# Four stages turned by DMA transposes instead of TensorE, in a fused recurrence and feed-forward kernel

## The chip, the cores and the metric

The kernel runs on one core of a Trainium2 chip. The metric is the device time of one execution in microseconds (us); lower is better. The value is the median over the timed runs.

## The reference

A linear recurrence with a decay per channel (an RWKV layer), followed by a feed-forward layer with a leaky ReLU:

```python
batch, n_heads, seq, head_dim = (4, 8, 768, 48)
for t in range(S):
    kt, vt, rt = (k[:, :, t].copy(), v[:, :, t].copy(), r[:, :, t].copy())
    cur = np.einsum('bhd,bhe->bhde', u[None] * kt, vt)
    y[:, :, t] = np.einsum('bhd,bhde->bhe', rt, state + cur)
    state = w[None, :, :, None] * state + np.einsum('bhd,bhe->bhde', kt, vt)
...
n_tokens, d_model, d_ff = (3072, 384, 2048)
h = x @ w_in
g = np.maximum(0.01 * h, h)
return (g @ w_out).astype(np.float32)
```

x is y with the heads side by side: 3072 tokens by 384 channels. Inputs and output are float32; the kernel computes in bfloat16 with float32 sums.

## The kernel before

The recurrence is computed in chunks of 128 tokens. There are 24 stages; stage n is chunk n // 4 of batch n % 4, so four neighbouring stages belong to four different batches, and stage n hands its state to stage n + 4. Each stage goes through these steps, and each step has a letter, by which an order of work written out by hand names it:

- r, k, v: loads of the stage's three inputs. GpSimd (POOL) issues them, converting to bfloat16, except stage 0's r and k (SP and ACT). wi and wo with a number are quarters of the two weight matrices, also issued by GpSimd.
- P (q or k): DVE multiplies r or k with a table of decay powers (qtab, ktab), giving the tile qk.
- The tile is turned so that channels lie on partitions (tile tp). Either TensorE (PE) does it, four matmuls against the identity for each half (T), and ACT or, with an @ behind the name, DVE copies the result from PSUM (t); or, with X and T around the number (X8T), one DMA transpose issued by SP does the whole stage.
- A: PE computes the products of q and k of a chunk into two PSUM banks. M (a or b): DVE masks one bank above the diagonal into the tile at.
- The diagonal (the term with u) has two forms. In the first, X without T multiplies the turned halves (prod) on DVE, D sums them over channels with wu on PE, Q scales v by the sums on DVE (vs), and Y begins with three matmuls of vs. M is then a multiplication by the mask. In the second, q is three DVE instructions (row_sums, which need the table u_tab), Q is two GpSimd instructions that put the sums on the diagonal of at, and M copies the products over it by predicate, so that it waits for Q; Y has no matmuls of vs.
- K: PE multiplies k and v. S: DVE makes the next state of it. Y: PE computes the stage's output, from stage 4 on with the state; y: ACT copies it to xT.
- G n.g and g n.g: a group of four blocks of the first feed-forward matrix for one stage on PE, and its activation on ACT. J m.j and j m.j: two blocks for a pair of stages. H and h: the second matrix for one stage on PE, its copy on ACT and its store by SP.
- F with a number: so many matmuls of ones on PE, without use for the result.

Before the change, stages 0 to 7 are turned by PE and have the first form of the diagonal (TURNED, DIAG = 8, 8); stages 8 and later use the transpose and the second form. The table u_tab is made from one row of u: SP loads the row, ACT converts it (u16), PE spreads it over partitions (U), ACT copies it (utab).

Everything up to stage 5's first feed-forward half is listed in ORDER, a string of these names. Each engine does its own steps in the order of that string, and a step waits by semaphore only for what it reads or overwrites. PSUM has 8 banks, handed out in rotation in the order of the list. After the list a loop runs over pairs of stages, m from 3 to 11: J for the pair m, then the sums and diagonals of the next but one pair, loads of later stages, P and transposes, H for the pair before, A, Y, M, K and S. The loop's text is the same for all stages.

GpSimd's queue matters here: it issues all loads but two and computes the diagonals of the second form, one after the other. SP's queue carries the transposes and stores.

Of the kernel before, what the change touches and what calls it, by code (L numbers as in the profile page):

```python
# [7 lines left out]
AF = mybir.ActivationFunctionType  # L8
AX = mybir.AxisListType
BF16 = mybir.dt.bfloat16  # L10
FP32 = mybir.dt.float32
# [6 lines left out]
HD = H * D  # L18
# [4 lines left out]
NSL = HD // 128  # L23

FIRST, NB, PACE = 6, B, 3
TURNED, DIAG, CARRY, EXACT = 8, 8, 4, 1
ORDER = """
w k0 r0 w8 u8 u wlz tcol k1 ones table one exps qk0 r1 v0z r5 F12 bc wi2 lnw id qtab wu8 v0 id8 u16 F13 Cm P0q ktab U
k3 P1q T0q Wl P0k utab T1q r3 P1k t0q T0k C P5q W T1k t1q@ k4 T5q t0k t1k@ tri t5q F2 A0 X0 v1 X1 F2 A1 M0a F3 D0 wi1
M0b F5 D1 F1 K0 k5 P3k P3q F11 T3k Q0 r4 F3 T3q P4k t3k F3 Y0 M1b v3 t3q T4k M1a y0 F2 K1 A3 r2 t4k Q1 F1 G0.2 M3a wi3  # L30
F1 Y1 S1 g0.2 G0.1 M3b v5 y1 X3 F2 G1.2 r7 P5k g0.1 S0 T5k g1.2 D3 P4q k6 G1.1 Q3 t5k T4q r6 g1.1 K3 P2q Y3 S3 t4q T2q
k2 X5 y3 F2 A5 X4 F1 A4 t2q M5a G3.2 v4 M4b F1 G3.3 wi0 g3.2 M4a D4 D5 G0.3 g3.3 k7 M5b G1.3 P7q g0.3 v7 Q5 K5 P6k G3.1
g1.3 S5 wo2 T6k g3.1 Y5 P6q v2 P2k t6k T6q Q4 y5 r10 F2 K4 T2k t6q@ T7q t2k Y4 v6 t7q@ A6 y4 S4 F1 A2 wo3 G1.0 M6a r11
F1 J2.7 P7k g1.0 M6b wo0 J2.0 j2.7 M2b J2.6 v8 j2.0 X2 M2a J2.2 j2.6 wo1 K7 J2.1 j2.2 v9 S7 K2 J2.4 j2.1 S2 r9 G0.0
P10q j2.4 r8 K6 J2.3 g0.0 S6 v11 D2 G3.0 j2.3 X6 Q2 k8 T7k g3.0 D6 J2.5 Q6 t7k k11 Y2 P11q j2.5 X7 A7 k9 y2 Y6 M7a k10
D7 M7b y6 G2.1 Q7 v10 G2.0 g2.1 G2.3 g2.0 G2.2 g2.3 H1 g2.2 P9q P8q H2 h1 P8k q8 X8T K8 H0 h2 P9k Q8 S8 X9T P10k P11k
K9 X10T H3 h0 q9 X11T S9 Q9 Y7 h3 A9 y7 A8 M8a M9a M9b M8b k12 r12 v12 k13 r13 v13
"""


# [4 lines left out]
class Sched:  # L45
# [7 lines left out]

    def add(self, eng, emit, R=(), W=(), dma=None):
        o = Op()
        o.eng, o.emit, o.dma, o.inc, o.val = eng, emit, dma, False, None
        deps = []
        for key in R:
            w = self.writer.get(key)
            if w is not None:  # L60
                deps.append((w, True))
        for key in W:
            w = self.writer.get(key)
            if w is not None:
                deps.append((w, False))
            for r in self.readers.get(key, ()):
                deps.append((r, False))
        o.deps = []
        for d, raw in deps:
            if d.dma is None and d.eng == eng and dma is None and (eng == "pe" or not raw):  # L70
                continue
            if d is not o and d not in o.deps:
                o.deps.append(d)
        for key in R:
            self.readers.setdefault(key, []).append(o)
        for key in W:
            self.writer[key] = o
            self.readers[key] = []
        self.ops.append(o)
        return o  # L80
# [47 lines left out]
def bass_rwkv5_eagle__then__act_leaky_relu_kernel(  # L128
# [13 lines left out]
    def SB(name, shape, dt=BF16):  # L142
        return ctx.enter_context(nc.sbuf_tensor(name, shape, dt))
# [5 lines left out]
    k_sb = SB("k_sb", [128, NST, HD])  # L149
    v_sb = SB("v_sb", [128, NST, H * E])  # L150
    w_row = SB("w_row", [128, HD // 2], FP32)
    u_row = SB("u_row", [1, HD], FP32)
    one_row = SB("one_row", [128, 128], FP32)
    u_row16 = SB("u_row16", [1, HD])
    w_head = SB("w_head", [H, D], FP32)
    u_head = SB("u_head", [H, D], FP32)
    wu_head = SB("wu_head", [H, D], FP32)
# [3 lines left out]
    lnw = SB("lnw", [128, HD], FP32)  # L161
    u_tab = SB("u_tab", [128, HD])
    k_f = SB("k_f", [128, EXACT, HD], FP32)
    r_f = SB("r_f", [128, EXACT, HD], FP32)
    qtab = SB("qtab", [128, HD])
    ktab = SB("ktab", [128, HD])
    tcol = SB("tcol", [128, 1], FP32)
# [4 lines left out]
    ones = SB("ones", [128, 128])  # L172
# [17 lines left out]
    V, A, PE, SP, G = nc.vector, nc.scalar, nc.tensor, nc.sync, nc.gpsimd  # L190
    sch = Sched(ctx, nc)
    add = sch.add
    free = list(range(8))

    def take():
        i = free.pop(0)
        return ps[i], ("ps", i)

    def give(key):
        free.append(key[1])  # L200

    def dram(h, offset, pattern):
        return bass.AP(tensor=h.tensor, offset=h.offset + offset, ap=pattern)
# [12 lines left out]
    def load_one(n, which, pace=()):  # L216
# [4 lines left out]
        else:  # L221
            dst = {"k": k_sb, "r": r_sb}[which][:, n, :].rearrange("p (h d) -> p h d", d=D)
        add("pool", lambda: G.dma_start(dst, src), R=pace, W=[(which, n)], dma=f"{which}{n}")  # L223

# [12 lines left out]
        add("pool", lambda: G.dma_start(w_out_sb[:, 4 * i:4 * i + 4, :], wout_view[:, 4 * i:4 * i + 4, :]),  # L237
            W=[("wout", i)], dma=f"wout{i}")

    def row(h):  # L240
        return dram(h, 0, [[HD, 1], [1, HD]])

    def by_head(h):
        return dram(h, 0, [[D, H], [1, D]])
# [11 lines left out]
    def fill(n):  # L256
# [6 lines left out]

        add("pe", emit, R=["ones"], W=[("ps", i), f"fill{n}"])

    def identity():
        add("pool", lambda: G.affine_select(ident[:, :], ones[:, 0:128], pattern=[[1, 128]], compare_op=ALU.is_equal,
                                            fill=0.0, base=0, channel_multiplier=-1), R=["ones"], W=["ident"])

# [52 lines left out]
        add("dve", lambda: V.tensor_tensor(wu_head[:, :], w_head[:, :], u_head[:, :], ALU.mult),  # L322
            R=["w_head", "u_head"], W=["wu_head"])

    def u_cast():
        add("act", lambda: A.activation(u_row16[:, :], u_row[:, :], AF.Copy), R=["u_row"], W=["u_row16"])

    def u_spread():
        ps_u, key = u_bank["u"] = take()
        add("pe", lambda: PE.matmul(ps_u[:, 0:HD], ones[0:1, 0:128], u_row16[:, :], start=True, stop=True),  # L330
            R=["ones", "u_row16"], W=[key])

    def u_table():
        ps_u, key = u_bank["u"]
        add("act", lambda: A.activation(u_tab[:, :], ps_u[:, 0:HD], AF.Copy), R=[key], W=["u_tab"])
        give(key)

    u_bank, c_bank = {}, {}
    at_bank, kv_bank, y_bank = {}, {}, {}

    def hd(x):
# [316 lines left out]
    def g2_out(n, c0=0, c1=HD):  # L658
# [14 lines left out]
            W=["w_row"], dma="w"),  # L673
        "w8": lambda: add("sp", lambda: SP.dma_start(w_head[:, :], by_head(w)), W=["w_head"], dma="w8"),
        "u8": lambda: add("sp", lambda: SP.dma_start(u_head[:, :], by_head(u)), W=["u_head"], dma="u8"),
        "u": lambda: add("sp", lambda: SP.dma_start(u_row[:, :], row(u)), W=["u_row"], dma="u"),
        "one": lambda: add("dve", lambda: V.memset(one_row[:, :], 1.0), W=["one_row"]),
        "tcol": tokens, "ones": filled, "exps": exponents, "v0z": zero_v, "qk0": zero_qk, "wlz": zero_w,
        "id": identity, "tri": triangle, "table": preload, "id8": small_identity, "wu8": wu_product,
        "bc": spread_w, "lnw": log_w, "qtab": lambda: table(qtab, qexp, "q"), "ktab": lambda: table(ktab, kexp, "k"),  # L680
        "Cm": columns_mm, "Wl": log_columns, "C": decay_columns, "W": decay_table,
        "u16": u_cast, "U": u_spread, "utab": u_table,
    }
    stage = {
        "P": lambda n, x: prep_half(n, half_of[x]), "T": lambda n, x: turn_mm(n, half_of[x]),
# [108 lines left out]
```

## Time and profile before

| | |
|---|---|
| median of the runs | 172.35 us (171.53 to 172.49, 3 runs) |
| span of the profiled execution | 168.6 us |
| its own time beside the span | not recorded; the span runs from the first to the last instruction, and the median is 3.75 us above it |
| PE busy | 163.7 us, 97% |
| DVE, ACT, POOL busy | 106.9, 90.8, 103.6 us |
| granted TensorE clock | 1.000 |

In the profile, PE is TensorE's matmuls, PEld its weight loads, DVE VectorE, ACT ScalarE, POOL GpSimd and SP SyncE; a q behind a name is the engine's issue queue. L with a number is a line of the kernel. A row of grouped instructions has line, engine, operation, output<-input, shapes and count, and behind the bar busy us, mean ns of one, and idle time of the engine before it with what ended it. A row of the chain has start, length and what. A row of the windows view has the window and its length, the busy time and count of PE, PEld, DVE, ACT and POOL in turn, then the granted clock, DMA packets in work (as a multiple of the 16 engines) and GB/s.

### The profile page before, as it was taken

To read this page: it belongs to the slowest core of one execution; us is meant where nothing else is said; L and a number is where in the kernel's file an instruction comes from. 1 tells how busy PE (TensorE), PEld (TensorE's weight loads), DVE (VectorE), ACT (ScalarE), POOL (GpSimd) and SP (SyncE) were. 2 spreads that over 40 slices of the span, in tenths; PEclk is the share of its full clock that TensorE was granted. 3 is DMA by queue.
4 is the path that set the end of the run, shared out by engine and by line. 5 is a ranking of instruction groups with operands and counts; after the bars stand their busy time and mean duration, and the time that the engine had idled before them with its cause. 6 is when DMAs were issued, how large, how long until landed. Compare 5 with 4: busy or idle time off the path is not lost.

```text
span 168.6 us, 5011 instructions
## 1 busy us (share of the span) xinstructions
PE 163.7 (97%) x2170; PEld 126.1 (75%) x2170; DVE 106.9 (63%) x217; ACT 90.8 (54%) x167; POOL 103.6 (61%) x117
## 2 busy tenths in 40 slices
PE   6899999999999999999999999999999999999994
PEld 4787898988667867867867867768768668668663
DVE  6599799874583999869959959969876050000000
ACT  3837866886123933933834735735637538449221
POOL 7999999990249998994993993993708100000000
PEclk9999999999999999999999999999999999999999
DMA  6999999999999959999599399299241011011012
GB/s 99 142 151 165 170 167 173 182 184 148 130 167 187 163 75 144 155 118 173 71 140 167 64 141 177 71 132 193 59 121 47 0 51 47 0 51 47 29 68 95
DMA packets 99148, 19.67 MB, mean 117 GB/s; under 512 B 92339, under 2 KB 99126, under 8 KB 99126
## 3 DMA queue, kind: packets, MB, share of 16 engines
q0 software_dynamic: 76512, 10.03, 92.1%
q1 hardware_dynamic: 21574, 9.12, 23.2%
q8 instruction: 17, 0.28, 0.7%
q10 hardware_dynamic: 1040, 0.20, 0.6%
q14 instruction: 5, 0.04, 0.1%
HBM read 20.45 MB, written 4.72 MB: 149 GB/s over the span
## 4 chain that ended last, share of the span: by engine, by line
PE 89%; POOL 5%; DMA 4%; issue 0%; ACT 0%; POOLq 0%
PE ps L652 37%; PE ps L628 31%; PE ps L605 6%; PE ps L566 6%; DMA w_in_sb<-in_moe_w_in_dram 4%; PE ps L432 4%; PE ps L473 2%; POOL k_sb L223 2%; POOL r_sb L223 2%; PE ps L407 1%; POOL v_sb L223 1%; PE ps L559 1%; PE ps L261 0%; POOL w_in_sb L233 0%; PE ps L460 0%
## 5 line engine op out<-in xcount | busy, mean ns | idle before, releaser
L652 PE MATMUL ps<-w_out_sb,gT 128*128 128x384 bf16 (+2 forms) x400 | 65.7, 320 | 0.0
L628 PE MATMUL ps<-xT,w_in_sb 128*128 128x256 bf16 x480 | 54.7, 273 | 0.0
L652 PEld LDWEIGHTS ps<-w_out_sb,gT 128*128 128x128 bf16 x400 | 37.9, 98 | 22.0
L393 POOL TENSOR_TENSOR at<-ident,s_tok 128x512 bf16<-128x512 bf16 x32 | 35.0, 1121 | 26.9 <-DVE s_tok L386 26.9
L628 PEld LDWEIGHTS ps<-xT,w_in_sb 128*128 128x128 bf16 x480 | 46.6, 98 | 6.4 <-ACT xT L580 0.2
L638 ACT ACTIVATE gT<-ps 128x512 bf16<-128x512 f32 x80 | 47.8, 597 | 6.4 <-PE ps L628 1.6
L664 ACT ACTIVATE out_sb<-ps 128x384 f32<-128x384 f32 (+2 forms) x25 | 11.9, 478 | 52.9 <-PE ps L652 52.9
L445 DVE CAST_PREDICATED at<-mask,ps 128x512 bf16<-128x512 uint16 x32 | 19.8, 684 | 18.0 <-PE ps L432 18.0
L223 POOL DMA_DIRECT2D v_sb<-in_v_dram x24 | 22.9, 955 | 0.0
L223 POOL DMA_DIRECT2D k_sb<-in_k_dram x23 | 21.5, 965 | 0.4 <-issue 0.4
L223 POOL DMA_DIRECT2D r_sb<-in_r_dram x23 | 21.2, 930 | 0.0
L353 DVE TENSOR_TENSOR qk<-r_sb,qtab 128x384 bf16<-128x384 bf16 x23 | 14.2, 617 | 3.8 <-DMA r_sb<-in_r_dram 3.8
L353 DVE TENSOR_TENSOR qk<-k_sb,ktab 128x384 bf16<-128x384 bf16 x23 | 13.0, 570 | 1.3 <-DMA k_sb<-in_k_dram 1.3
L580 ACT ACTIVATE xT<-ps 128x384 bf16<-128x384 f32 x24 | 11.0, 491 | 4.8 <-PE ps L566 4.8
L605 PE MATMUL ps<-xT,w_in_sb 128*128 128x128 bf16 x192 | 12.5, 219 | 0.4 <-DMA w_in_sb<-in_moe_w_in_dram 0.4
L615 ACT ACTIVATE gT<-ps 128x512 bf16<-128x512 f32 x16 | 9.6, 597 | 5.3 <-PE ps L605 4.9
L605 PEld LDWEIGHTS ps<-xT,w_in_sb 128*128 128x128 bf16 x192 | 11.0, 98 | 0.8 <-DMA w_in_sb<-in_moe_w_in_dram 0.5
L384 DVE TENSOR_TENSOR rku<-r_sb,ku 128x384 bf16<-128x384 bf16 x16 | 10.8, 675 | 0.6
L566 PE MATMUL ps<-at,v_sb 128*32 128x128 bf16 x384 | 10.8, 220 | 0.0
L534 DVE TENSOR_TENSOR sum_t<-ps,st 128x384 bf16<-128x384 f32 x16 | 8.8, 551 | 2.7 <-PE ps L473 2.7
L441 DVE TENSOR_TENSOR at<-ps,mask 128x512 bf16<-128x512 f32 x16 | 10.3, 681 | 0.3 <-PE ps L432 0.3
L261 PE MATMUL ps<-ones 128*128 128x128 bf16 x69 | 8.5, 257 | 1.3 <-DVE ones L251 1.3
(60 smaller groups left out, 135.1 us busy)
## 6 DMA issues: line engine op xcount, KB each, us to landing
out_dram<-out_sb SPq DMA_DIRECT2D x23, 192.0 KB, 3.6
v_sb<-in_v_dram POOLq DMA_DIRECT2D x24, 96.0 KB, 6.3
k_sb<-in_k_dram POOLq DMA_DIRECT2D x23, 96.0 KB, 6.1
r_sb<-in_r_dram POOLq DMA_DIRECT2D x23, 96.0 KB, 5.9
w_in_sb<-in_moe_w_in_dram POOLq DMA_DIRECT2D x4, 384.0 KB, 6.8
w_out_sb<-in_moe_w_out_dram POOLq DMA_DIRECT2D x4, 384.0 KB, 9.3
tp<-qk SPq DMA_TRANSPOSE x16, 2.8
k_f<-in_k_dram ACTq DMA_DIRECT2D x1, 192.0 KB, 2.7
```

Source lines behind the costliest of these rows:

```text
L223: add("pool", lambda: G.dma_start(dst, src), R=pace, W=[(which, n)], dma=f"{which}{n}")
L353: add("dve", lambda: V.tensor_tensor(qk[iq][:, H * half:H * half + H, 0:D], hd(src), hd(tab[:, :]), ALU.mult), R=[(name, n), "qk"[half] + ...
L384: add("dve", lambda: V.tensor_tensor(rku[i2][:, :], r_of(n), ku[i2][:, :], ALU.mult), R=[("r", n), ("ku", i2)], W=[("rku", i2)])
L393: add("pool", lambda hh=hh, s_of=s_of: G.tensor_tensor(at[ia][:, hh, :, :], ident[:, :].unsqueeze(1).to_broadcast([128, NP, 128]), s_of.un ...
L445: add("dve", lambda: V.copy_predicated(at[n % NAT][:, hh, :, :], mask[:, :].bitcast(mybir.dt.uint16).unsqueeze(1).to_broadcast([128, NP, 1 ...
L566: last = PE.matmul(ps_y[32 * q:32 * q + 32, 128 * s:128 * s + 128], a, m, start=not whole and step == 0, stop=step == len(columns[q]) - 1)
L580: add("act", lambda: A.activation(xT[m % NX][:, :, 128 * half:128 * half + 128], ps_y[:, 0:HD].rearrange("p (s t) -> p s t", t=128), AF.Copy),
L605: last = PE.matmul(ps_g[:, 128 * f:128 * f + 128], w_in_sb[:, s, 128 * fb:128 * fb + 128], xT[ix][:, s, t], start=s == 0, stop=s == NSL - 1)
L628: last = PE.matmul(ps_g[:, 256 * f:256 * f + 256], w_in_sb[:, s, 128 * fb:128 * fb + 128], xT[ix][:, s, :], start=s == 0, stop=s == NSL - 1)
L638: add("act", lambda: A.activation(gT[ig][:, 2 * j:2 * j + 2, :].rearrange("p f t -> p (f t)"), ps_g[:, :], AF.Prelu, alpha=0.01), R=[key], ...
L652: last = PE.matmul(ps_o[:, 0:c1 - c0], gT[ig][:, s, 128 * half:128 * half + 128], w_out_sb[:, s, c0:c1], start=s == 0, stop=s == NFB - 1)
L664: add("act", lambda: A.activation(out_sb[io][:, c0:c1], ps_o[:, 0:c1 - c0], AF.Copy), R=[key], W=held)
```

## The change

Stages 4 to 7 are turned by DMA transposes (TURNED 4), and take the second form of the diagonal (DIAG 4). u_tab is loaded whole, 128 rows of u in one converting transfer that GpSimd issues, so that u_row, u_row16, u16, U and utab go. The list is written anew, for all stages in it. The loop and the functions of the steps stay.

```diff
-TURNED, DIAG, CARRY, EXACT = 8, 8, 4, 1
+TURNED, DIAG, CARRY, EXACT = 4, 4, 4, 1
 ORDER = """
-w k0 r0 w8 u8 u wlz tcol k1 ones table one exps qk0 r1 v0z r5 F12 bc wi2 lnw id qtab wu8 v0 id8 u16 F13 Cm P0q ktab U
-k3 P1q T0q Wl P0k utab T1q r3 P1k t0q T0k C P5q W T1k t1q@ k4 T5q t0k t1k@ tri t5q F2 A0 X0 v1 X1 F2 A1 M0a F3 D0 wi1
-M0b F5 D1 F1 K0 k5 P3k P3q F11 T3k Q0 r4 F3 T3q P4k t3k F3 Y0 M1b v3 t3q T4k M1a y0 F2 K1 A3 r2 t4k Q1 F1 G0.2 M3a wi3
-F1 Y1 S1 g0.2 G0.1 M3b v5 y1 X3 F2 G1.2 r7 P5k g0.1 S0 T5k g1.2 D3 P4q k6 G1.1 Q3 t5k T4q r6 g1.1 K3 P2q Y3 S3 t4q T2q
-k2 X5 y3 F2 A5 X4 F1 A4 t2q M5a G3.2 v4 M4b F1 G3.3 wi0 g3.2 M4a D4 D5 G0.3 g3.3 k7 M5b G1.3 P7q g0.3 v7 Q5 K5 P6k G3.1
-g1.3 S5 wo2 T6k g3.1 Y5 P6q v2 P2k t6k T6q Q4 y5 r10 F2 K4 T2k t6q@ T7q t2k Y4 v6 t7q@ A6 y4 S4 F1 A2 wo3 G1.0 M6a r11
-F1 J2.7 P7k g1.0 M6b wo0 J2.0 j2.7 M2b J2.6 v8 j2.0 X2 M2a J2.2 j2.6 wo1 K7 J2.1 j2.2 v9 S7 K2 J2.4 j2.1 S2 r9 G0.0
-P10q j2.4 r8 K6 J2.3 g0.0 S6 v11 D2 G3.0 j2.3 X6 Q2 k8 T7k g3.0 D6 J2.5 Q6 t7k k11 Y2 P11q j2.5 X7 A7 k9 y2 Y6 M7a k10
-D7 M7b y6 G2.1 Q7 v10 G2.0 g2.1 G2.3 g2.0 G2.2 g2.3 H1 g2.2 P9q P8q H2 h1 P8k q8 X8T K8 H0 h2 P9k Q8 S8 X9T P10k P11k
-K9 X10T H3 h0 q9 X11T S9 Q9 Y7 h3 A9 y7 A8 M8a M9a M9b M8b k12 r12 v12 k13 r13 v13
+w k1 ones qk0 one F15 bc r0 tcol wlz v0z exps r1 k0 k2 table lnw r2 k3 ktab qtab r3 w8 P1k P1q P0q id F26 T1q P0k v1 T1k u8 id8 t1q@ wu8 t1k@ F8 Cm
+wi2 P2q Wl P3k F11 T3k t3k T2q P2k T0q t0q C A1 tri P3q T3q T2k t3q X1 W v3 M1b M1a D1 v0 T0k t0k A3 Q1 F8 Y1 X3 D3 t2q A0 M3b M3a t2k F9 A2 Q3 F4 Y3
+y1 M0a X0 wi1 v2 X2 r4 u G1.2 M2b k4 D0 Q0 y3 G3.2 g1.2 K0 K1 D2 G1.1 M0b Y0 y0 G3.1 M2a Q2 wi3 S1 Y2 P4k g3.2 P4q X4T K3 S3 G0.2 q4 y2 g3.1 G2.1 r5
+P5q G0.1 k5 P5k X5T g2.1 G2.2 g0.2 wi0 v5 q5 G1.3 g0.1 g1.3 G0.3 g2.2 v4 wo0 S0 A4 G3.3 G2.3 wo2 G0.0 wo1 wo3 Q4 M4a Q5 g0.3 M4b G1.0 A5 K2 g3.3 g1.1
+g0.0 k6 Y4 M5a r6 y4 G3.0 M5b r7 K5 K4 S4 Y5 S2 k7 g1.0 S5 r8 P6k P6q q6 G2.0 P7k P7q q7 X6T k8 y5 J2.6 J2.1 X7T J2.2 q8 P8k P8q g2.0 J2.5 k9 r9 v8
+j2.1 J2.4 X8T J2.0 q9 J2.7 k10 k11 j2.6 H1 v7 r10 P9q j2.2 g2.3 H0 v6 Q6 P9k X9T P10k j2.5 A6 j2.4 j2.7 g3.0 H3 A7 h1 v9 H2 M6b j2.0 Q7 M7a K8 M6a Y6
+K9 h0 M7b P10q X10T h3 r11 Q8 Q9 h2 v13 K6 Y7 k13 A8 y6 v10 y7 r12 S8 J2.3 v11 A9 S6 j2.3 r13 k12 M8a M8b P11q M9a v12 P11k M9b K7 S7 X11T S9
 """
...
-    u_row = SB("u_row", [1, HD], FP32)
...
-    u_row16 = SB("u_row16", [1, HD])
...
-    def row(h):
-        return dram(h, 0, [[HD, 1], [1, HD]])
+    def rows(h):
+        return dram(h, 0, [[0, 128], [1, HD]])
...
-    def u_cast():
-        add("act", lambda: A.activation(u_row16[:, :], u_row[:, :], AF.Copy), R=["u_row"], W=["u_row16"])
-
-    def u_spread():
-        ps_u, key = u_bank["u"] = take()
-        add("pe", lambda: PE.matmul(ps_u[:, 0:HD], ones[0:1, 0:128], u_row16[:, :], start=True, stop=True),
-            R=["ones", "u_row16"], W=[key])
-
-    def u_table():
-        ps_u, key = u_bank["u"]
-        add("act", lambda: A.activation(u_tab[:, :], ps_u[:, 0:HD], AF.Copy), R=[key], W=["u_tab"])
-        give(key)
+    def load_u():
+        add("pool", lambda: G.dma_start(u_tab[:, :], rows(u)), W=["u_tab"], dma="u")
...
-        "u": lambda: add("sp", lambda: SP.dma_start(u_row[:, :], row(u)), W=["u_row"], dma="u"),
+        "u": load_u,
...
-        "u16": u_cast, "U": u_spread, "utab": u_table,
```

More of the change, by code (lines that the diff above doesn't have):

```diff
@@ L323, in wu_product @@
             R=["w_head", "u_head"], W=["wu_head"])
-    def u_cast():
-        add("act", lambda: A.activation(u_row16[:, :], u_row[:, :], AF.Copy), R=["u_row"], W=["u_row16"])
-    def u_spread():
-        ps_u, key = u_bank["u"] = take()
-        add("pe", lambda: PE.matmul(ps_u[:, 0:HD], ones[0:1, 0:128], u_row16[:, :], start=True, stop=True),
-            R=["ones", "u_row16"], W=[key])
-    def u_table():
-        ps_u, key = u_bank["u"]
-        add("act", lambda: A.activation(u_tab[:, :], ps_u[:, 0:HD], AF.Copy), R=[key], W=["u_tab"])
-        give(key)
-    u_bank, c_bank = {}, {}
+    def load_u():
+        add("pool", lambda: G.dma_start(u_tab[:, :], rows(u)), W=["u_tab"], dma="u")
+    c_bank = {}
     at_bank, kv_bank, y_bank = {}, {}, {}
```

## The prediction

> **What bounds the kernel now.** I read the page first, then the chain of waits in order of time, then busy time by stretch.
>
> ```profile
> span 168.6 us, 5011 instructions
> ...
> PE 163.7 (97%) x2170; PEld 126.1 (75%) x2170; DVE 106.9 (63%) x217; ACT 90.8 (54%) x167; POOL 103.6 (61%) x117
> ...
> DMA  6999999999999959999599399299241011011012
> ...
> q0 software_dynamic: 76512, 10.03, 92.1%
> q1 hardware_dynamic: 21574, 9.12, 23.2%
> ```
>
> PE is busy throughout, and in the first half of the span so are the DMA engines. The chain (start, length, what) says from when PE is the bound:
>
> ```profile
> 16.34 0.84 PE ps L605 x12
> ...
> 21.18 0.78 PE ps L605 x12
> ...
> 22.01 0.67 PE ps L605 x12
> ...
> 25.06 0.22 PE ps L407 x4
> 25.28 0.17 PE ps L559 x3
> ...
> 37.02 0.34 PE ps L566 x16
> ...
> 46.55 0.17 PE ps L473 x4
> 46.72 2.60 PE ps L652 x16
> ...
> 52.76 0.55 PE ps L432 x16
> ...
> 53.36 5.41 PE ps L628 x48
> ...
> 61.93 0.90 PE ps L566 x56
> ```
>
> From 16.34 on the chain stays on PE. At 53.36 the loop begins (L628, 48 matmuls of the pair m=3). Two stretches of the windows view, cut there:
>
> ```profile
> 16.34:53.36 37.02, 36.97 (x608) 30.04 (x609) 26.74 (x62) 21.37 (x40) 27.46 (x32) 1.00 1.80 168
> 53.36:168.60 115.24, 112.95 (x1368) 84.94 (x1368) 67.30 (x118) 59.98 (x109) 60.84 (x63) 1.00 0.89 97
> ```
>
> In the list's stretch PE is busy 36.97 of 37.02 us, and DMA packets overlap 1.8 deep; behind it DMA falls to 0.89. The change leaves the loop's text alone, and there PE has the least slack. So I compare one moment: when PE ends the list, 53.36 now. What moves it moves the end by as much. The profiled span is 168.6 and the median of the runs 172.35; I take the 3.75 between them as unchanged and add the difference to the median.
>
> **The change, part by part.**
>
> *PE's list, if nothing waits.* Removed: 8 turns T (four of L407, 0.22 each, 1.76 together), 4 products D and u's spread (about 0.5 together, at most what T costs for as many matmuls), 4 times the vs matmuls (L559, 0.17 each, 0.69): about 3 us. Fills rise from 69 to 81, but all of the new list's stand ahead of its first G (G1.2), inside waits. From G1.2 on the new list holds 16 G (0.67: 10.72), 8 J (5.41), 4 H (2.60: 10.40), 6 A (0.55 is two: 1.65), 10 K (0.17: 1.70), Y0 and Y2 (0.17+0.34 each: 1.02), Y4 to Y7 (0.90 is two: 1.80) and two D (0.3): 33.0. ACT loses 8 copies of turns and two steps of u's table, and idles there anyway (21.37 of 37.02 us busy). A change of shape costs more than these rows (L605 took 0.78 behind an A, 0.67 elsewhere), so I add 1.0: 34.0.
>
> *When G1.2 starts.* It stands behind Y3 on PE, and Y3 behind Q3 on DVE. DVE's prices, with the row sums and GpSimd's for later:
>
> ```profile
> L441 DVE TENSOR_TENSOR at<-ps,mask 128x512 bf16<-128x512 f32 x16 | 10.3, 681 | 0.3 <-PE ps L432 0.3
> ...
> L375 DVE TENSOR_TENSOR vs<-v_sb,ps 128x384 bf16<-128x384 bf16 x8 | 4.3, 546 | 0.4 <-DMA v_sb<-in_v_dram 0.4
> L393 POOL TENSOR_TENSOR at<-ident,s_tok 128x512 bf16<-128x512 bf16 x4 | 4.2, 1072 | 9.6 <-DVE s_tok L386 9.6
> ...
> L353 DVE TENSOR_TENSOR qk<-r_sb,qtab 128x384 bf16<-128x384 bf16 x11 | 3.9, 353 | 3.3 <-DMA r_sb<-in_r_dram 3.3
> ...
> L233 POOL DMA_DIRECT2D w_in_sb<-in_moe_w_in_dram x4 | 3.2, 794 | 0.0
> L368 DVE TENSOR_TENSOR prod<-tp 128x512 bf16<-128x512 bf16 x8 | 3.2, 417 | 0.0
> L419 DVE CAST tp<-ps 128x512 bf16<-128x512 f32 x4 | 2.7, 688 | 0.1
> ...
> L386 DVE TENSOR_REDUCE s_tok<-rku 128x8 f32<-128x384 bf16 x2 | 1.1, 553 | 0.1
> L384 DVE TENSOR_TENSOR rku<-r_sb,ku 128x384 bf16<-128x384 bf16 x2 | 0.7, 358 | 0.1
> L382 DVE TENSOR_TENSOR ku<-k_sb,u_tab 128x384 bf16<-128x384 bf16 x2 | 0.7, 350 | 0.0
> ```
>
> The timeline has ACT's first table end at 5.38; in the new list ktab is the first, and P1k starts then:
>
> ```profile
> 4.77 0.61 ACT L315 ACTIVATE qtab<-lnw,qexp 128x384 bf16<-128x384 f32 x1
> ```
>
> From P1k to Q3 DVE has 4 masks (2.72), 2 casts (1.38), 6 short P (2.12), stage 0's two P (taken like L375, 1.1), 2 X (0.83), 2 Q (1.1) and four small ones (an estimate, 1.2): 10.5, so Q3 ends near 15.9; the small overlap of neighbours I set against the waits for r1 and for A1 and A3. Y3 takes 0.51: G1.2 starts at 16.4 (15.7 to 17.4). With no further wait the list ends at 16.4+34.0 = 50.4.
>
> *DVE.* Added, 4 row sums (0.35+0.36+0.55 = 1.26 each, 5.0); gone, 4 X and 4 vs (0.96 each, 3.9) and two casts (1.4). Even, with 10 us idle in that stretch (26.74 of 37.02): nothing on the path.
>
> *Transposes X4T to X7T.* Two windows of tile tp, each with one transpose, the first from 60.8 with no load beside it, the second from 62.2 with loads:
>
> ```profile
> DMA to landing us min/median/max: 2.7/2.7/2.7
> ```
> ```profile
> DMA to landing us min/median/max: 5.8/5.8/5.8
> ```
>
> X4T goes out when P4q is done: 5.3 us of DVE work (4 masks, 2 X, 2 Q, a state, 2 P) behind Q3, 21.2. All loads are under way then, so I take 5.8 (from 2.7): it lands at 27.0. A4 is due on PE after 11 G, 3 K, 2 Y and 2 D, 9.2 us past G1.2, at 25.6. PE waits 1.4 there; the list would end at 51.8. On SP the transposes X4T to X9T stand ahead of the first store, h1's, which then waits for P9k; with four output buffers nothing waits for that store before the loop. The predicated masks M4 to M7 are priced like L441 and now wait for Q4 to Q7 on GpSimd too; Q4 ends near 26, before A4 does.
>
> *GpSimd's queue and the loads.* This decides. POOL issues every load in order. The window of k_sb with four loads from 33.4 to 36.0, then the first load (1.4), then v_sb's at 36.8, then v_sb's at 66.0:
>
> ```profile
> L223 POOL DMA_DIRECT2D k_sb<-in_k_dram x4: 1079/1092/1107, 33.4 to 36.0; - x4
> ...
> DMA to landing us min/median/max: 9.6/9.9/10.2
> ```
> ```profile
> DMA to landing us min/median/max: 4.3/4.3/4.3
> ```
> ```profile
> DMA to landing us min/median/max: 9.5/9.5/9.5
> ```
> ```profile
> DMA to landing us min/median/max: 6.3/6.3/6.3
> ```
>
> A load lands 4.3 after its issue when nothing is ahead of it. POOL issues one per 0.87 (three in 33.4 to 36.0), and in a full queue they land every 0.66 (43.6 to 45.6). By 36.8+9.5 = 46.3 the queue has landed 34 stage loads and 8 weight transfers. In the new list v6 is behind 29 loads, u's table and the 8 weights: four loads fewer (2.6) and u more (0 to 0.66, the bytes of a load in longer runs; 0.5), so 44.2. POOL's own side: 30 loads at 0.87, 8 weights and u at 0.79, Q4 and Q5 (four halves at 1.07, 4.3) and 2 of small work and of waiting for s4: issue ends near 40.9, landing 45. Q4 and Q5 hide under the queue, just.
>
> What no row shows is the cost c that a transpose lays on loads queued with it. Five are ahead of v6 (X4 to X8; in the list of before, one at the queue's very end). Upper end: the load at 66.0 landed 2.0 late beside one transpose and a store; slower issue had given back 5 times 0.2 by then, so 3.0 in all; the store holds two loads' bytes, 1.3: c is 1.7, or 2.0 if the store is cheaper. Lower end: q1 is busy 23.2% of the span against 92.1% for q0, 39.1 to 155.3 us. q0's 42 transfers landed in 40.6 us, its other 36 loads at 0.66 come to 23.8: it overlaps 2.4 deep, and q1's 39.1 at that depth is 16.3 for 16 transposes and 25 stores, at most 1.0 per transpose. If the loads fill every gap, 0. I take 1.5, between the two rows. Then v6 lands at 44.2+5(1.5) = 51.7 and v9, next on the queue behind Q6, at 52.4. PE reaches Y6 at 49.1 (51.8 less 2.7 for Y6 and what is behind it) and waits. Behind K9 stand K6, Y7, A8, J2.3, A9 and K7, 2.3 with K9 itself: the list ends at 54.7, 1.3 later than now. A4's wait disappears in this one. **172.35+1.3 = 173.7.**
>
> The Trainium skill has a rule against the change ("DMA: Bandwidth & Descriptors", section "Issuing engines are not separate DMA queues"): DMAs from SP and from GpSimd run on the same 16 engines and interleave. The trace agrees, with 5.8 for 2.7. By the rule c is above 0 and the sum goes toward 173.7; if the queues were independent, it would be 170.8.
>
> **The rivals.**
> *The loads fit, and PE alone sets the list's end (faster).* c is below 1.0. For it: the lower row, and DMA that idles after 46.3. Against it: five transposes in the fullest stretch. It gives 51.8, or 170.8; with X4T at 2.7 as well, 50.4, or 169.4. It decides as long as v6 lands before 49.1. At c = 1.23 the list ends where it does now.
> *GpSimd becomes the bound.* Q4 waits for s4, and behind it wait k6 and all later loads, so a late row sum moves every landing. For it: POOL has only 1 us to spare against the queue. Against it: k4, r4 and u go out ten transfers ahead of Q4. If s4 is 3 us later than taken, v6 lands at 48 at the earliest; the queue has emptied by then, and only X6 to X8 add their 1.5 each: 52.5, end 55.5, 174.5.
> *The transposes cost the full 2.0.* v6 at 54.2, end 57.2: 176.2.
>
> **How the numbers follow.** About 0.5% (0.86 us) is what a measurement of this kernel can tell from no change. Slower by that asks for c above 1.4: 0.40, of which 0.10 for 2.0 and more; GpSimd's queue: 0.08; slower together 0.48. Within 0.5%, c from 1.05 to 1.4: 0.20. The loads fit, or c stays under 1.05: 0.32. The likeliest case's own range is 173.2 to 175; the range of 8 in 10 leaves out X4T at 2.7 and c of 2.0 and over: 169.9 to 176.0.
>
> **What would show it.** In the changed profile: 32 turning matmuls of 64 and 12 of the vs kind of 24; a first G near 16.4; PE idle late in the list before a Y or K, with v_sb's load as releaser; loads issued near 35 that take over 11 us to land; the loop's first pairs at 54 to 56. Wrong, if PE is unbroken from about 17 and the loop begins before 52, or if PE waits for masks that wait for GpSimd's diagonals, instead of for loads.

## The result, and the profile after

The changed kernel takes 183.33 us (median; 182.41 to 184.61), the kernel before 172.42 us on the same chip (171.53 to 172.77). The ratio is 1.0675, with a 95% interval from 1.0611 to 1.0739. The forecast was 173.7, with a range to 176.0: slower, but by far more than expected. Here and below, executions more than 1.5% above the fastest of their kernel are left out of the ratios but not of the medians (in e4, e9 and e11), and the profile of e4 is of such an execution.

The lines of the page that answer to those of before:

```profile
span 182.8 us, 4926 instructions
...
PE 164.8 (90%) x2121; PEld 126.2 (69%) x2121; DVE 113.4 (62%) x219; ACT 85.6 (47%) x159; POOL 112.8 (62%) x126
...
PE   6995990299999799599999999999999999999994
...
PEclk9999997569999999999999999999999999999999
DMA  7999999999999999999993997959933102011022
...
q0 software_dynamic: 76656, 10.13, 103.3%
q1 hardware_dynamic: 25796, 10.17, 29.2%
```

PE is busy 164.8 us, about as long as before (163.7), in a span that is 14.2 us longer. The PE row shows a hole in slices 7 and 8 (from the span's start, 4.6 us each), and the clock row shows that the granted clock falls there. The chain in order of time (start, length, what) names what filled the hole:

```profile
15.64 9.37 DMA r_sb<-in_r_dram
...
25.03 2.27 DVE qk L338 x2
...
27.33 13.58 DMA tp<-qk
...
41.04 0.40 PE ps L417 x8
...
44.62 4.66 PE ps L613 x42
...
66.86 8.65 DMA tp<-qk
...
75.65 0.40 PE ps L417 x8
```

Before, the chain stayed on PE from 16.34 on. Now a load (stage 5's r), two products of VectorE and one transpose of 13.58 us (stage 5's) carry it to 41.04. PE's waits in the first 80 us (engine, line, releaser; total, times, longest):

```profile
PE ps L417 <- DMA tp<-qk: 10.9, 3, 8.4
PE ps L544 <- DVE vs L360: 1.8, 1, 1.8
...
PE ps L551 <- ACT out_sb L649: 0.9, 1, 0.9
```

L417 is step A. It waits for stage 4's transpose, 8.4 us, for stage 5's, 0.3, and inside the loop for stage 11's, 2.2. Stage 5's wait is short only because PE is already late by then: the chain runs through that transpose and not through stage 4's, so by these times stage 4's alone on time would have left PE waiting at A5, which stands 48 matmuls behind A4. The transposes of stages 4 and 5 by the view of their tile, and w_out's four transfers, sent just ahead of them:

```profile
L343 SPq DMA_TRANSPOSE tp<-qk x1: 1387/1387/1387, 23.1 to 23.1; - x1
...
DMA to landing us min/median/max: 12.1/12.1/12.1
```
```profile
L343 SPq DMA_TRANSPOSE tp<-qk x1: 2765/2765/2765, 27.3 to 27.3; - x1
...
DMA to landing us min/median/max: 13.6/13.6/13.6
```
```profile
L232 POOL DMA_DIRECT2D w_out_sb<-in_moe_w_out_dram x4: 785/792/802, 20.0 to 22.2; - x4
...
DMA to landing us min/median/max: 16.1/19.0/21.0
```

By stretches (window, its length, busy time of PE, PEld, DVE, ACT and POOL, then the granted clock, DMA share, GB/s): from the first G to the loop, the wait for stage 4, the stretch of the low clock (which begins inside that wait), and the loop:

```profile
18.22:65.08 46.86, 37.16 (x558) 29.36 (x551) 33.90 (x61) 17.91 (x35) 36.83 (x40) 0.89 2.18 144
27.00:35.38 8.38, 0.03 (x2) 0.03 (x1) 1.95 (x5) 0.97 (x2) 6.84 (x9) 0.67 1.46 153
29.90:40.20 10.30, 4.82 (x49) 4.66 (x50) 1.29 (x2) 1.31 (x3) 10.30 (x12) 0.50 1.94 151
65.08:182.80 117.72, 113.11 (x1372) 85.00 (x1369) 67.00 (x124) 60.21 (x110) 58.90 (x61) 1.00 0.97 100
```

The loop begins at 65.08 and not at 53.36: 11.7 us of the 14.2. The other 2.5 lie in the loop, 2.2 of them the wait for stage 11's tile. The clock is 0.50 for 10.3 us: it falls at 29.90, 2.9 us into the hole, and stays low for 4.8 us behind it. What those 4.8 us cost shows in the timeline, in 48 equal matmuls of the first feed-forward matrix, after and before:

```profile
35.92 4.86 PE L590 MATMUL ps<-xT,w_in_sb 128*128 128x128 bf16 x48
```
```profile
38.51 2.84 PE L605 MATMUL ps<-xT,w_in_sb 128*128 128x128 bf16 x48
```

4.86 us instead of 2.84: 2.0 us more.

### The profile page after: what moved, and what is told of

Same layout as the page of the kernel before. It is cut to its first block, busy times and chain, and to the rows that moved or that the text cites. A ratio compares the mean times of both kernels' runs of the same rounds, so it can differ in the third digit from the quotient of the medians.

```text
span 182.8 us, 4926 instructions
## 1 busy us (share of the span) xinstructions
PE 164.8 (90%) x2121; PEld 126.2 (69%) x2121; DVE 113.4 (62%) x219; ACT 85.6 (47%) x159; POOL 112.8 (62%) x126
## 4 chain that ended last, share of the span: by engine, by line
PE 66%; DMA 17%; POOL 8%; DVE 6%; issue 1%; ACT 0%; POOLq 0%
PE ps L637 32%; PE ps L613 25%; DMA tp<-qk 12%; DMA r_sb<-in_r_dram 5%; PE ps L551 4%; DVE qk L338 3%; PE ps L417 2%; DVE at L430 2%; POOL k_sb L218 2%; POOL r_sb L218 2%; POOL v_sb L218 2%; PE ps L458 2%; POOL w_in_sb L228 1%; PE ps L590 1%; DVE sum_t L519 1%
## 5 line engine op out<-in xcount | busy, mean ns | idle before, releaser
L378 POOL TENSOR_TENSOR at<-ident,s_tok 128x512 bf16<-128x512 bf16 x40 | 43.6, 1114 | 31.7 <-DVE s_tok L371 31.6
L613 PEld LDWEIGHTS ps<-xT,w_in_sb 128*128 128x128 bf16 x480 | 46.8, 98 | 6.4
L430 DVE CAST_PREDICATED at<-mask,ps 128x512 bf16<-128x512 uint16 x40 | 25.1, 683 | 26.3 <-PE ps L417 26.3
L417 PE MATMUL ps<-tp 48*128 48x128 bf16 x192 | 8.7, 221 | 11.0 <-DMA tp<-qk 10.9
L338 DVE TENSOR_TENSOR qk<-k_sb,ktab 128x384 bf16<-128x384 bf16 x23 | 14.9, 654 | 5.3 <-DMA k_sb<-in_k_dram 5.3
L338 DVE TENSOR_TENSOR qk<-r_sb,qtab 128x384 bf16<-128x384 bf16 x23 | 17.4, 758 | 1.0 <-DMA r_sb<-in_r_dram 0.9
L417 PEld LDWEIGHTS ps<-tp 48*128 48x128 bf16 x192 | 5.6, 95 | 15.0 <-issue 13.6
L590 PE MATMUL ps<-xT,w_in_sb 128*128 128x128 bf16 x192 | 14.0, 239 | 0.0
L369 DVE TENSOR_TENSOR rku<-r_sb,ku 128x384 bf16<-128x384 bf16 x20 | 12.9, 647 | 0.7
L590 PEld LDWEIGHTS ps<-xT,w_in_sb 128*128 128x128 bf16 x192 | 12.8, 109 | 0.6 <-issue 0.2
L371 DVE TENSOR_REDUCE s_tok<-rku 128x8 f32<-128x384 bf16 x20 | 11.1, 553 | 0.7
```

Of the source, the lines that this page charges most:

```text
L338: add("dve", lambda: V.tensor_tensor(qk[iq][:, H * half:H * half + H, 0:D], hd(src), hd(tab[:, :]), ALU.mult), R=[(name, n), "qk"[half] + ...
L369: add("dve", lambda: V.tensor_tensor(rku[i2][:, :], r_of(n), ku[i2][:, :], ALU.mult), R=[("r", n), ("ku", i2)], W=[("rku", i2)])
L378: add("pool", lambda hh=hh, s_of=s_of: G.tensor_tensor(at[ia][:, hh, :, :], ident[:, :].unsqueeze(1).to_broadcast([128, NP, 128]), s_of.un ...
L417: last = PE.matmul(at_bank[n][hh][0][:, 128 * p:128 * p + 128], tp[it][rows, NP + p, :], tp[it][rows, p, :], start=True, stop=True)
L430: add("dve", lambda: V.copy_predicated(at[n % NAT][:, hh, :, :], mask[:, :].bitcast(mybir.dt.uint16).unsqueeze(1).to_broadcast([128, NP, 1 ...
L590: last = PE.matmul(ps_g[:, 128 * f:128 * f + 128], w_in_sb[:, s, 128 * fb:128 * fb + 128], xT[ix][:, s, t], start=s == 0, stop=s == NSL - 1)
```

## The experiments

The theories were these. T: the transposes are sent into a queue full of loads and take 12 to 14 us, and TensorE waits. R1: GpSimd's diagonals wait for row sums and hold up the loads behind them. R2: the new list is worse by itself, whatever turns the stages; T3 is the form of R2 that blames w_out's early transfers. Every kernel was timed against the kernel before on the same chip. "Loop" is where the first loop pair starts on PE in its profile (before 53.36, after 65.08); kernels as fast as before have it up to 55.4, so differences under 2 us in that column say nothing. In the quoted expectations the kernels carry these names with a suffix.

| kernel | median us (before) | ratio, 95% | loop |
|---|---|---|---|
| e1: after, 4 and 5 turned by PE | 177.69 (171.97) | 1.033, 1.029 to 1.037 | 59.84 |
| e2: after, 4 to 7 turned by PE | 178.51 (171.97) | 1.037, 1.032 to 1.042 | 61.67 |
| e3: after, old diagonal | 183.71 (171.97) | 1.067, 1.062 to 1.072 | 67.03 |
| e4: after, w_out later | 182.38 (171.97) | 1.052, 1.046 to 1.058 | 64.76 |
| e5: the new list alone | 179.97 (171.08) | 1.051, 1.046 to 1.057 | 62.99 |
| e6: before, 4 to 7 by transposes | 192.23 (171.08) | 1.120, 1.112 to 1.127 | 75.67 |
| e7: e2, four loads ahead of diagonals | 177.73 (171.08) | 1.039, 1.034 to 1.043 | 60.80 |
| e8: e7, those loads ahead of w_out | 176.27 (172.21) | 1.026, 1.018 to 1.034 | 56.23 |
| c3: e8, v3 earlier | 176.02 (172.21) | 1.026, 1.019 to 1.032 | 57.63 |
| e9: after, loads ahead of w_out | 181.60 (172.21) | 1.053, 1.043 to 1.063 | 63.76 |
| e10: before, w_out ahead | 179.00 (172.20) | 1.043, 1.037 to 1.048 | 62.35 |
| e11: before, one unread transpose | 172.13 (172.20) | 1.002, 0.998 to 1.006 | 55.05 |
| c1: before, 7's diagonal new | 170.67 (171.08) | 0.997, 0.993 to 1.001 | 54.98 |
| c4: before, 6's and 7's new | 171.81 (172.20) | 0.999, 0.995 to 1.003 | 55.40 |
| c5: c4, GpSimd's step later | 171.55 (170.98) | 1.002, 1.000 to 1.005 | 54.52 |

**Stages 4 and 5 turned by TensorE (e1).**

```diff
-... P4q X4T ... P5k X5T ... v5 q5 G1.3 ... wo2 G0.0
+... P4q ... P5k ... v5 q5 T4k T4q t4k t4q G1.3 ... wo2 T5k T5q t5k t5q G0.0
```

> The changed kernel, with stages 4 and 5 turned by TensorE again (32 matmuls and four evictions by ScalarE in place of two transposes); diagonal, u's table, loads and the rest of the list as changed. Theory T (the transposes, sent into a queue full of loads and w_out's transfers, come 12 to 14 us later and TensorE stands idle for the first of them): the wait at A4, 8.4 us, and the half clock after it go, TensorE pays some 2.5 us for the turning, and the time is 172 to 177. Rival R1 (GpSimd's diagonals of stages 4 and 5 wait for VectorE and hold up the loads behind them): they stay, so the time stays at 180 to 184. Rival R2 (the order of the new list brings the first G and the first weights late, whatever turns a stage): 179 to 184.

The ratio falls from 1.0675 to 1.033, some 5.9 us. The long wait and its hole are gone; L418, step A here, waits for transposes twice, 2.4 us in all, for stages 6 or later:

```profile
PE ps L418 <- DMA tp<-qk: 2.4, 2, 1.9
```

T is right for these 5.9 us. The median is 0.7 above T's range, and 5.7 us of loss stay, so T is not the whole cause.

**Stages 4 to 7 turned by TensorE (e2).**

```diff
-... X6T k8 ... q8 P8k P8q g2.0 J2.5 ... X7T
+... T6k T6q t6k t6q k8 ... q8 P8k P8q g2.0 T7k t7k T7q t7q J2.5 ...
```

> The changed kernel, with stages 4 to 7 all turned by TensorE again; diagonal by GpSimd, u's casting transfer and the list's order stay. T: 170 to 176, since the loop's first pair of stages is not late for a turned tile any more; within 2 us of the kernel that turns 4 and 5 alone on TensorE, because the transposes of stages 6 and 7 were waited for by 0 to 1 us at most. R1: 178 to 184, GpSimd's waits at its diagonals being as before. R2: 178 to 184.

178.5, the same as e1 within the intervals, as T expected of stages 6 and 7; the level was missed by 2.5 us. PE now waits 3.4 us for stage 6's product, whose row r6 came late. That gave the next two suspects: GpSimd's waits ahead of r6's load, and the list.

**The old diagonal, transposes kept (e3).**

```diff
-TURNED, DIAG, CARRY, EXACT = 4, 4, 4, 1
+TURNED, DIAG, CARRY, EXACT = 4, 8, 4, 1
-... q4 ... q5 ... Q4 M4a Q5 ...
+... X4 A4 ... X5 A5 K2 g3.3 D4 Q4 ... D5 Q5 ...        (6 and 7 likewise)
```

> The changed kernel, with the diagonal of stages 4 to 7 in the old form (product, four small matmuls, VectorE's scaled v, three matmuls in Y; mask by multiplication), and the transposes left in. GpSimd then only issues loads in the list. T: A4 still waits 7 to 10 us for its transpose and the time is 180 to 185. R1: the loads k6 and after go out up to 6 us earlier, and the time is 172 to 177. R2: 180 to 185.

No difference from the changed kernel (1.067 for 1.0675). A4 waits 7.9 us, with GpSimd free of the diagonals of stages 4 to 7. R1 is not what made the change slow.

**w_out's transfers later (e4).**

```diff
-... v4 wo0 S0 A4 ... wo2 G0.0 wo1 wo3 Q4 ... r8 ...
+... v4 S0 A4 ... G0.0 Q4 ... r8 wo0 wo1 wo2 wo3 ...
```

> The changed kernel, with the four transfers of w_out moved behind r8's load on the load queue, so that the transposes of stages 4 and 5 share the DMA engines with loads of small packets only. T, if it is the large weight packets that the transposes alternate with: the transposes of stages 4 and 5 take 5 to 7 us, A4's wait falls under 2 us, and the time is 174 to 178 (the transposes of 6 and 7 may meet w_out instead and take 10 or more). T, if any queued load does it: those two still take over 10 us and the time is 181 to 185. R1: the diagonals hold the loads as before, 181 to 185. R2: 179 to 185.

Between the two forms of T: in the profiled execution the two transposes took 7.6 and 4.5 us, and A4 waited 4.7. The queue had emptied at 30, when the first one landed. H then waited 4.6 us for w_out, so the total says little; the latencies say that transposes are slow among loads, and slower among w_out's transfers.

**The new list alone (e5).** Everything else of the change undone: PE turns, the old diagonal, u by its row.

> The new list with nothing else of the change: stages 4 to 7 turned by TensorE, their diagonal in the old form, u's table by the row, its spreading matmul and two ScalarE steps. It stands to the kernel of e2_turn4567_pe (178.5) as the old diagonal and the old u path. Theory T2 (what is left of the loss, once TensorE turns, comes from GpSimd: its diagonals of stages 4 and 5 wait for VectorE's row sums and hold back r6's load, for which TensorE then waits 3.4 us): 171 to 175. Rival R2 (it is the order of the list: loads, weights and steps in a worse order, whatever does the diagonal): 176 to 180.

180.0, a ratio of 1.051. T2 falls: the list alone is 5% slower. From e5 to e2, the new diagonal and u's transfer gain 1.5%, so they help in that list.

**The old list, with stages 4 to 7 turned by transposes (e6).**

```diff
-... P4q ... T4k ... t4k ... T4q ... t4q ...
+... P4q X4T ...                                  (5 to 7 likewise)
```

> The kernel before, list and all, with the turning of stages 4 to 7 alone done by a DMA transpose each, issued right behind the product that it reads. T: here too the transposes stand in a queue of loads and w_out's transfers, take 8 to 14 us each, and TensorE waits for the first of them: 178 to 188. R2: the transposes cost the old list little, 170 to 174.

192.2, slower than the change itself and than T's range. Step A waits three times:

```profile
PE ps L430 <- DMA tp<-qk: 16.9, 3, 7.4
```

In the old list the transposes of stages 4 to 7 cost 12%; in the new one, from e2 to the changed kernel, 3%. Behind the first two of them the loads landed 5.3 us later than before, behind three 8.3.

**Four loads ahead of the diagonals (e7).**

```diff
-... wo1 wo3 Q4 M4a Q5 ... k6 ... r6 ... r7 ... k7
+... wo1 wo3 k6 r6 r7 k7 Q4 M4a Q5 ...
```

> The kernel of e2_turn4567_pe (178.5), with four loads (k6, r6, r7, k7) issued on GpSimd's queue ahead of the diagonals of stages 4 and 5 instead of behind them. T2: r6 comes some 4 us earlier, the 3.4 us wait of TensorE before stage 6's turning goes, and so does the half clock behind it: 173 to 176. R2: 177 to 180.

R2: 177.7, as e2 within the intervals. The loads went out from 22.9 on and not from 29.4, yet r6 landed as late, for it stood behind w_out. The wait stays:

```profile
37.40 0.61 PE L393 MATMUL ps<-ident,qk 128*128 128x128 bf16 x4 [3.51 <-DVE qk L339]
```

**The same loads ahead of w_out (e8).**

```diff
-... v4 wo0 S0 A4 G3.3 G2.3 wo2 ... wo1 wo3 k6 r6 r7 k7 Q4
+... v4 k6 r6 r7 k7 wo0 S0 A4 G3.3 G2.3 wo2 ... wo1 wo3 Q4
```

> The kernel of e7_turn_pe_loads_first (177.7: the changed kernel with stages 4 to 7 turned by TensorE), with the same four loads (k6, r6, r7, k7) moved once more, ahead of the four transfers of w_out. Theory T3 (what the new list loses by itself is that w_out's four transfers, 9.7 us of the queue, stand ahead of stage 6's rows: TensorE waits 3.5 us to turn stage 6, 1.1 us for the next pair, and runs some 5 us at a lower clock behind that): r6 lands near 30 and not 37.7, those waits go, the first pairs come 5 to 6 us earlier, and the time is 170.5 to 173.5. Rival R2b (the new list loses in many places, its beginning above all, where the first G starts at 16.9): 174.5 to 178.

r6's load now took 8.1 us to land, instead of 13.9:

```profile
34.63 0.67 PE L393 MATMUL ps<-ident,qk 128*128 128x128 bf16 x8 [1.36 <-DVE qk L339]
```

The wait falls by 2.1 us, the clock stays at full, and the loop starts 4.6 us earlier. The ratio falls from 1.039 to 1.026. T3's direction and its step are right; its level is missed, and 2.6% stay, as R2b expected.

**v3 earlier (c3).** v3's load ahead of wi2, the filler F4 out.

> The kernel of e8_loads_before_wout, with v3's load issued ahead of w_in's first transfer instead of behind it, and without the four filling matmuls ahead of stage 3's output. T3 with the beginning as a second, smaller loss: TensorE's 0.6 us wait before Y3 goes and the first G starts 0.3 to 0.8 us earlier, so 0.3 to 0.8 us faster than that kernel, about even with the kernel before or up to 1 us faster. If the beginning is bound elsewhere: no difference from that kernel (within 0.3 us).

No difference from e8 in time. But the edit did not do what it was meant to: the first G came at 17.7, and at 16.3 in e8. So it does not show whether the list's beginning holds what is left of the loss.

**The changed kernel, the same loads ahead of w_out (e9).** The edit of e8 in the changed kernel.

> The changed kernel with all four stages turned by transposes, and the same four loads ahead of w_out's transfers. T and T3 together: A4 still waits, since its transpose still stands in a full queue, 4 to 8 us; stage 6's rows were no wait here (TensorE was late already), so it gains only what the smaller packets beside the transposes bring: 178 to 183. If the order of the loads were the whole loss and the transposes none: 170 to 174.

181.6, as T expected: stage 4's transpose took 8.7 us among loads (12.1 in the changed kernel), and A4 still waits 5.6. It landed at 31.3 and not at 35.2; now A5 waits 2.2 us for stage 5's transpose, which took 11.4 and landed at 38.2.

**One transpose that nobody reads, in the old list (e11).**

```diff
+tp_spare = SB("tp_spare", [128, 2 * NP, 128])
-... P4q k6 ...
+... P4q Z4 k6 ...      (Z4: dma_start_transpose of stage 4's qk into tp_spare)
```

> The kernel before with one transpose added that nobody reads: stage 4's products into a spare tile, issued behind the product, near 18.8 us, into the full load queue; TensorE still turns stage 4 itself. T: it takes 6 to 10 us from issue to landing (2.7 to 2.8 where the queue is empty) and every load queued behind it lands 2 to 3 us later than before (the forecast's price was 1.5, with 2.0 as its end); the time grows by 0 to 4 us, as some step waits for a late load. If a transpose beside loads cost only its own 2.7 us of an empty machine's time shared over the queue: loads 1 to 1.5 us late, and the time within 1 us of before.

This is the disputed price by itself. The transpose, and then the last load of the list:

```profile
L362 SPq DMA_TRANSPOSE tp_spare<-qk x1: 1429/1429/1429, 18.4 to 18.4; - x1
...
DMA to landing us min/median/max: 8.2/8.2/8.2
```
```profile
L222 POOL DMA_DIRECT2D v_sb<-in_v_dram x1: 1077/1077/1077, 36.9 to 36.9; - x1
...
DMA to landing us min/median/max: 12.0/12.0/12.0
```

The same load took 9.5 before (the prediction quotes it; it was issued 0.1 earlier). So with one transpose ahead of it a load sent 18 us later took 2.5 us longer. All loads from wi0 (sent at 20.1) to this one landed 2.6 to 2.7 later than before; k6's and r6's, sent 1.8 and 0.9 us ahead of the transpose, landed 2.5 later too. These are two single executions; c1 and the kernel before, which have the same loads and no such transpose, differ by 0.4 there. The time does not change within its interval, 1.002: TensorE waited once, 1.4 us, for stage 6's product.

**w_out ahead of stage 6's rows in the old list (e10).**

```diff
-k6 ... r6 ... wo2 v2 ... wo3 r11 ... wo0 ... wo1
+wo2 wo3 wo0 wo1 k6 ... r6 ... v2 ... r11 ...
```

> The kernel before, list and all, with the four transfers of w_out moved ahead of k6's load on the load queue, where the new list has them, and nothing else. T3: the loads of stages 6 and 7 and all behind land 7 to 8 us later, TensorE waits for stage 6's and 7's tiles, and the time grows by 3 to 8 us (175 to 180). If the order of those loads is harmless in a tuned list too: within 1 us of before.

179.0, 4.3% slower by moving four transfers. r6's load takes 11.8 us and not 6.5, and PE waits 5.1 us at stage 6's turn:

```profile
32.11 0.58 PE L405 MATMUL ps<-ident,qk 128*128 128x128 bf16 x4 [5.08 <-DVE qk L351]
```

T3's mechanism stands, in both directions.

**The diagonal alone, in the old list (c1, c4, c5).** These look for a version that beats both.

```diff
-TURNED, DIAG, CARRY, EXACT = 8, 8, 4, 1
+TURNED, DIAG, CARRY, EXACT = 8, 7, 4, 1          (c1; 6 in c4 and c5)
-... X7 A7 ... M7a ... D7 M7b ... Q7 v10 ... H1
+... A7 ... v10 q7 Q7 ... H1 M7a M7b
-... v6 ... A6 ... M6a ... M6b ... X6 ... D6 ... Q6       (c4)
+... q6 v6 Q6 ... A6 ... M6a ... M6b ...                  (c4; in c5 Q6 behind wo1, the masks later)
```

> The kernel before, with stage 7's diagonal alone in the new form (row sums by VectorE, diagonal by GpSimd behind its last load of the list, mask by predicated copy), everything else as before. If the new form is free where GpSimd is idle and nothing waits (T2): four small matmuls and three of 128 columns go, 0.4 us of TensorE's time, so 0.1 to 0.6 us faster than before. If GpSimd's step slows VectorE down beside it and that shows (rival): 0.3 to 1.5 us slower.

> The kernel before, with the diagonals of stages 6 and 7 in the new form (GpSimd's step of stage 6 between two loads, that of stage 7 behind its last), turning by TensorE, nothing else. Eight small matmuls and six of 128 columns go, 0.8 us of TensorE's time. If TensorE's work is what counts there: 0.3 to 0.9 us faster than before. If stage 6's masks, which wait for GpSimd, or VectorE's steps, which are slower beside GpSimd's, hold TensorE up: 0.3 to 2 us slower.

> The kernel of c4_before_diag67 (stages 6 and 7 with the diagonal by GpSimd), with GpSimd's step of stage 6 issued behind w_out's last transfer, and stage 6's masks later with it. If the 2.05 us wait for w_out was what ate the gain: the wait goes, and it is 0.4 to 2 us faster than before. If the masks then come late for stage 6's output, or VectorE's slower steps show: within 0.4 us of before, or slower.

c1 and c4 show no difference that can be told from none, and c5 is at best even. In c4 GpSimd waited for stage 6's sums with w_out's transfers behind it, and TensorE waited for the last of them:

```profile
POOL at L391 <- DVE s_tok L384: 2.8, 1, 2.8
PE ps L650 <- DMA w_out_sb<-in_moe_w_out_dram: 2.0, 1, 2.0
```

So R1's mechanism exists, though it did not decide the change. In c5 that wait is gone, and still nothing is gained; where the 0.8 us of saved matmuls went is open. No version here is faster than the kernel before beyond its interval.

## Why the prediction was wrong, by its own steps

Slower was right, and so was the cause in kind, transposes and loads in one queue; the path was another. The prediction put the loss on v6's load and Y6. It came at A4 and A5, which waited for the transposes themselves, and from losses of the new list for which the prediction had no term.

The sizes, from the ratios, one step upon the other: the new list alone +5.1%, the new diagonal and u's transfer -1.5%, stages 6 and 7 by transposes -0.4%, stages 4 and 5 by transposes +3.5%. Together 6.75%. Each has some 0.7% of uncertainty, and the parts lean on each other: the same diagonal gains nothing beside the transposes (e3).

- *The comparison at the list's end* held for 11.7 of 14.2 us. That the rest moves the end by as much, and no more, was wrong: the loop's wait for stage 11's tile (2.2) is for a transpose sent at 66.86, among the list's last loads, which now went out from 59.9 to 66.0; it took 8.65 us, where stage 11's took 4.7 before. e8, without the transposes of stages 4 to 7, has 1.4 us of that wait too.
- *PE's list, 34.0 us of work,* was nearly right. From 18.22 to 65.08 PE is busy 37.16 us, 2.0 of it through the low clock: 35.2 without.
- *G1.2 at 16.4 (to 17.4)* came at 18.2: VectorE waited 2.2 us for v3's load. In e2, e7, e8 and e9, which begin in the same way, it came at 16.3 to 17.0.
- *The transposes X4T and X5T* are the step that failed most. Stage 4's was sent at 23.1 (forecast 21.2, in a sum whose items reach 5.3 without the state that it names) and took 12.1 us (5.8), so A4 waited 8.4 and not 1.4. Stage 5's had no price at all; it was sent at 27.3, behind r5's load, took 13.6, and is the one on the chain. The row of 5.8 came from the loop, where a few loads were in flight; the argument had said itself that here all loads are under way, and still took that row. Its bounds, 2.7 to 5.8, did not hold the value. (The row of 2.7 had a load sent at 61.6 beside it after all; another before, at 48.3 with none, took 2.7 too.) e1 shows 5.9 us for the two together; how they share it no run shows.
- *The clock* had no term. 8.4 us without matmuls halved it for 10.3 us: 2.0 us. The Trainium skill ("TensorE: Matmul & The Clock Gate", Part 1) says that an idle window of some 3.4 us brings the half rate; the trace agrees in the half rate, 0.50, but not in the length: the clock fell 2.9 us into this wait, and in e1 a wait of 1.9 us was enough. A wait that long is thus dearer than its length.
- *c, the price of a transpose on the queue,* was taken as 1.5, with 2.0 as its end. It is some 2.6 (e11; e6's first two give 5.3 together). The overlap of q0's and q1's shares, from which the lower end came, mixed stretches with full and empty queues. The Trainium skill's rule in "DMA: Bandwidth & Descriptors", section "Issuing engines are not separate DMA queues", pointed the right way: they interleave.
- *Y6 waits for v6's load* was the wrong wait. PE was already later than the load. It waited at A4, for a transpose, and at Y6 0.9 us for ScalarE.
- *Q4 and Q5 hide under the queue* was right in its result, not in its reason: GpSimd waited 1.96 and 1.54 us for sums there, and taking the diagonals out (e3) or the loads past them (e7) changed little. v6's load went out at 42.0 (forecast 40.9).
- *The order of the new list* was taken as harmless but for v6 and v9. The prediction did not ask when stage 6's row lands, behind four transfers of w_out; e10 prices that at 4.3% in the old list, e8 at some 1.3% in the new one, and e9 at some 1.4% in the changed kernel itself. The new list as a whole, 5.1%, weighs more than the transposes of stages 4 and 5, 3.5%; w_out's place is the part of it that is shown. What else the new list loses, 2.6% with the diagonal's gain inside, is open: e8's first G still starts 1.7 us later than the old list's first, and three waits of 1.3 to 1.4 us are left in its profile.
- *VectorE even: nothing on the path* was wrong, with a small effect. In the list the short products with r took 970 ns on average, where the prediction's row has 353. Stage 5's two, beside GpSimd's diagonal of stage 4, took 2.27 us together and stand on the chain. In e3, without that diagonal, they took 0.36 each and the transpose went out at 25.7 and not 27.3; it landed only 1.0 us earlier, and the time was the same.

```profile
L338 DVE TENSOR_TENSOR qk<-r_sb,qtab 128x384 bf16<-128x384 bf16 x7 | 6.8, 970 | 0.2 <-DMA r_sb<-in_r_dram 0.2
```

Of the signs that it named, the counts were right (32 turning matmuls, 12 of the vs kind), and the loads issued near 35 did take over 11 us to land (12.8). The first G was 1.8 late, the loop's first pairs came at 65 and not at 54 to 56, and PE idled before an A, with a transpose as releaser, and not before a Y or K with v_sb's load.

## What to carry to other kernels

A transpose sent to a queue that is full takes the time of the queue, not its own: price it from a row with the same queue ahead of it, and ask which engine stands idle until then, and what its clock does afterwards. When an order of loads is written anew, look up for every early consumer when its load lands in the new queue; a few large transfers ahead of a small one that is needed soon cost 4.3% in the old list here, and some 1.4% in the changed kernel. And test a list without the feature, and the feature without the list, before judging either.

## What the runs showed of the hardware

- One transpose of 128 by 1024 took 2.7 us from issue to landing alone, 7.6 to 8.7 in a queue of loads (e4, e6, e9, e11), 11.3 as the second of two there (e6), and 11.4 to 14.2 with w_out's transfers around it (the changed kernel, e3, the second of e9). It put some 2.6 us on the loads queued with it (e11), where a load in a full queue takes 0.66. The Trainium skill ("Advanced Engine Details and Errata", section "X-Bar Transpose (TRN2)") calls transposes as fast as regular DMAs. In latency the traces agree: 2.7 alone beside 4.3 for a load alone, and in the changed kernel's full queue 12.1 and 13.6 beside 15.9 and 15.2 for v5's and v4's loads, sent at 18.2 and 19.1.
- A wait of 8.4 us on TensorE left the granted clock at 0.50 for 10.3 us; single waits of 1.4 (e8) and 2.0 us (c4) left it at 1.00, but with waits of 1.9 (e1) and 2.2 us (e9) it fell to 0.50 for 3.4 us, and in e7 it fell 1.9 us into a wait of 3.5.
- VectorE's short two-input products took 970 (r) and 750 ns (k) on average in the changed kernel's list, and 352 before. Single ones in the changed kernel took 0.35 us where GpSimd ran no tensor_tensor beside them, and 1.15 to 1.2 where it ran one for 1 us or more; one took 3.0. (One in e2 took 1.2 with none beside it.)
